# Attention, MLP and routed experts on one core: the sixth pair's product turned, and another order of the first batch's side work

## The chip, the cores and the metric

The kernel runs on one core of a Trainium2 chip. The metric is the device time of one execution in microseconds; the median of three runs of the kernel before is 1160.09 us (1159.63 to 1160.9). Lower is better.

## What is computed

The reference has three stages, one after the other, on 4 batches of 448 tokens:

```
q_n, k_n = rmsnorm(q, g_q), rmsnorm(k, g_k)              # 4 batches, 12 heads, 448 tokens, 64 wide
attn = softmax(q_n @ k_n.T / 8) @ v                      # heads laid side by side: 1792 tokens x 768
h = attn @ w_in;  x = (h * clip(h + 3, 0, 6) / 6) @ w_out    # 768 -> 2048 -> 768, both weights in float64
# capacity routing: every token to one of 8 experts, 224 tokens each
out[tokens of e] = relu(x @ w1[e]) @ w2[e]
```

The two MLP weights come as 64-bit floats and have to be narrowed to 32 bits on the chip. Products that need full precision are made of a high and a low part of each operand.

## The kernel before

**Attention by pairs.** The 48 heads are worked off in 24 pairs, six to a batch; the code counts them from 0, so the sixth pair of the first batch is i = 5. A pair goes through these steps, each a small function: `load` (q and k by DMA), `squares` (ACT, L251), `fold` (POOL, L256, adds the halves of the squares), `sums` (DVE, L267), `guess` (DVE) and `invert` (Newton steps for the inverse root, L279 to L282 on POOL, 12 instructions for a group of two pairs), `norm` (POOL, L298), `transp` (TensorE transposes L315, then `qh` and `kh` on ACT, L324, and the low parts `ql` and `kl` on DVE, L327), `s1` (scores, L338) with the row maxima `mx` on DVE (L341), `mt` (the maxima are transposed, L347, and spread as `mr` on DVE, L349), `sT` (scores transposed, less the maxima, L360) with the exponentials `ph` on ACT (L371).

**Two forms of the last product.** The product with v exists in two forms. In the turned one (`pv`, L449, and `psums`) the exponentials stream 448 wide, the result is copied to `xn_t` on ACT (L452), and the row sums `sm` come from extra matmuls (`L460` in the first batch; in later batches from sums `pa` that POOL adds beforehand, L442 and L465). The sums then make a trip through DRAM: `rs_out` writes `sum_dr`, `rs_in` reads it back as `rs`, `rec` makes the reciprocal `rr` on DVE (L482, L483), `r_out` writes `rec_dr`, `r_in` reads it spread over the partitions into `rb`, `xmul` multiplies on POOL (L497), and `xsplit` gives the high part on ACT (`xh`, L507) and the low part on POOL (`xl`, L505). In the other form (`av`, L400, named QMAJOR) 112 columns of exponentials are the weights and 66 columns stream; the sum falls out of an extra column, `normalize` divides on POOL (L421), and `xt` transposes back (L432). Before, the sixth and the last pair take this form.

**The weights.** `conv` narrows one of 16 column blocks of w_in: part -1 loads it (`wraw`, 768 KB), part 0 is on ACT (L141), parts 1 to 3 on DVE (L142 to L144, `cv`), and a last part stores it (`w<-cv`, 384 KB). The first MLP matrix (`mlp1_atoms`, L559) reads it back as `win_v`, splits it on ACT (L118) and on POOL or DVE (L119), keeps the split for later batches (`w_hl`), and multiplies; `g` leaves through L562 and L564.

**The order.** Nothing is scheduled by a planner. Every step is entered with a number by `at(t, fn, ...)`; the numbers are sorted, and each engine gets its instructions in that order. One pair is 16 places long. MLP matmuls are filled in between from a queue, evenly over the places left of a batch. All DMAs named here go through one queue, SP's, which also issues in that order and holds everything behind a DMA that waits. The constants T_..., TX0 and QMAJOR (L68 to L81) and the loop at L746 to L796 are the whole table.

```
    for i in range(NH // 2):
        t = 16 * i
        at(t + T_LOAD, load, i)
        first = 16 * g[0]
        t_sq = first + T_SUMS + 4 * (i - g[0])
        at(t_sq, squares, i)
        ...
            at(first + (T_INV0 if late_g else T_INV), invert, g)
```

Of the kernel before, what the change touches and what calls it, by code (L numbers as in the profile page):

```python
# [21 lines left out]
def kernel(  # L22
# [15 lines left out]
    B, H, S, D = q.shape  # L38
# [7 lines left out]
    NP = H // 2  # L46
# [21 lines left out]
    CI, CI0, CI1, CI2, CO = 6, 1.75, 2.5, 0.5, 1.5  # L68

    T_LOAD, T_VLOAD, T_NORM, T_Q, T_K, T_V = -72, -12, -38, -30, -28, 6  # L70
    T_SUMS, T_INV, T_INV0, NG0 = -50, -42, -35.5, 10
    T_S1, T_MT = (-24, -23.9, -16, -15.9), -9
    T_ST = (0, 0.1, 8, 8.1)
    T_AV = ((17, 18, 19.5, 20.5), (22, 23, 24.5, 25.5))
    T_NUM, T_XT, T_MLP = 28, 33, (37, 41, 41, 37)
    T_ADD, T_PV, T_SUM = (6, 13), (15.6, 15.62, 15.64, 15.66), 15.7
    T_RS, T_RL, T_REC, T_RO, T_RB, T_X, T_XH, T_XL = 19.5, 21.5, 24, 25.5, 28, 33, 35.5, 39.5
    GD, WD2, C_ST = 12, 8, 5
    TX0 = (20, 23, 27, 29, 32.5, 39, 42, 46)
    QMAJOR = (NP - 1, B * NP - 1)  # L80
    T_CI, D_CI, T_CO, D_CO, T_CL = 20, 10, 180, 12, 14  # L81


    order = ExitStack()
# [652 lines left out]
    def at(t, fn, *args):  # L737
        events.append((t, len(events), fn, args))
# [6 lines left out]

    for i in range(NH // 2):  # L746
        t = 16 * i
        at(t + T_LOAD, load, i)
        at(t + T_VLOAD, vload, i)
        g = GROUP[i]  # L750
        first = 16 * g[0]
        t_sq = first + T_SUMS + 4 * (i - g[0])
        at(t_sq, squares, i)
        if 2 <= i < NG0:
            at(t_sq + 2, fold, i)
            t_sq += 3
        at(t_sq, sums, i)
        late_g = 4 <= g[0] < NG0
        if i == g[-1]:
            at(t_sq if 2 <= i < NG0 else first + T_INV, guess, g)  # L760
            at(first + (T_INV0 if late_g else T_INV), invert, g)
        at(t + (T_INV0 + 0.1 if late_g and i == g[0] else T_NORM), norm, i)
        at(t + T_Q, transp, i, 0)
        at(t + T_K, transp, i, 1)
        at(t + T_V, vsplit, i)
        for c in range(NCH):
            at(t + (T_S1[c] if i else -24 + 0.1 * c), s1, i, c)
            at(t + (T_ST[c] if i else (-9, -8.9, 1, 1.1)[c]), sT, i, c)
            if i in QMAJOR:
                for s in range(2):  # L770
                    at(t + T_AV[s][c], av, i, s, c)
            else:
                at(t + T_PV[c], pv, i, c)
        at(t + (T_MT if i else -21), mt, i)
        if i in QMAJOR:
            at(t + T_NUM, normalize, i)
            at(t + T_XT, xt, i)
        else:
            for n in range(2 if i >= NP else 0):
                at(t + T_ADD[n], padd, i, n)  # L780
            at(t + T_SUM, psums, i)
            tx = TX0 if i < NP else (T_RS, T_RL, T_REC, T_RO, T_RB, T_X, T_XH, T_XL)
            for d, fn in zip(tx, (rs_out, rs_in, rec, r_out, r_in, xmul)):
                at(t + d, fn, i)
            at(t + tx[6], xsplit, i, False)
            at(t + tx[7], xsplit, i, True)
        if (i + 1) % NP == 0:
            at(t + T_MLP[i // NP], mlp_next, i // NP)
# [1 line left out]
    at(8 * H + 2, prefetch, 0)  # L790
    at(8 * H + 14, prefetch)
    for u in range(NF if wide else 0):
        for out_, t in ((0, T_CI + D_CI * u), (1, T_CO + D_CO * u)):
            at(t - T_CL, conv, (out_, u), -1)
            for part in (0, 1, 2, 3, C_ST):
                at(t + part, conv, (out_, u), part)  # L796
# [446 lines left out]
    for pi, (t, hfs) in enumerate(passes):  # L1243
# [10 lines left out]
        for f in range(NF):  # L1254
            i, k = divmod(f, QF)
# [139 lines left out]
```

## Time and profile before

| | |
|---|---|
| median of three runs | 1160.09 us |
| profiled execution | 1162.06 us, its span 1160.2 us |
| busy: TensorE (PE), DVE, ACT, POOL | 95%, 60%, 45%, 40% |
| granted TensorE clock, mean | 0.979 |
| first 58 us: PE busy | 40.42 us |
| 600 us to the end: PE busy | 540.93 of 560.20 us |

The profile is one execution. A row of the view by stretches gives each engine's busy time in that stretch, the granted TensorE clock as a share of 2.4 GHz, and how busy the DMA engines were. A row of the timeline gives start, length, engine, line, what is written and read and how many, and in square brackets the idle time of that engine just before, with what ended it. The trace keeps two records for one 32-bit product of `av` or `sm`, so x16 there are 8 products and x64 are 32.

### The profile page before, as it was taken

The numbers are of one execution on the slowest core, as the hardware profiler recorded it, in microseconds if no ns is written. First come the engines' busy times: TensorE is split into PE (matmuls) and PEld (weight loads), VectorE is DVE, ScalarE is ACT, GpSimd is POOL, SyncE is SP. The second block draws the span as 40 slices with busy tenths as digits, with TensorE's granted clock in tenths as the row PEclk, the third lists the DMA queues.
The fourth block names the chain that finished last, engine by engine and source line by source line (L and its number), as shares of the span: only waits on it lengthen the run. The fifth ranks groups of instructions, "written<-read, shape, count | busy, mean of one in ns | idle before, by whom it ended". The sixth has DMA issues, their size and how long they took to land.

```text
span 1160.2 us, 19232 instructions
## 1 busy us (share of the span) xinstructions
PE 1099.2 (95%) x7073; PEld 880.7 (76%) x7073; DVE 692.2 (60%) x1440; ACT 521.3 (45%) x941; POOL 464.6 (40%) x410
## 2 busy tenths in 40 slices
PE   4978899999999999999999999999997999999997
PEld 3446556766766667787767888888887899999997
DVE  7877877886677845212341666666665846555550
ACT  4655555745545556533542111111114766666551
POOL 4665555664445533112444000000004677775540
PEclk9987989999999999999999999999998999999999
DMA  4575998978777887659996222222237888877731
GB/s 133 145 197 148 248 300 252 309 238 297 251 250 253 257 288 239 222 190 276 356 310 204 78 69 82 64 76 71 70 104 185 245 262 247 248 227 217 226 130 39
DMA packets 215357, 232.17 MB, mean 200 GB/s; under 512 B 28296, under 2 KB 188384, under 8 KB 215264
## 3 DMA queue, kind: packets, MB, share of 16 engines
q1 hardware_dynamic: 211936, 219.94, 61.6%
q0 software_dynamic: 3328, 11.01, 3.1%
q8 instruction: 55, 0.90, 0.3%
q14 instruction: 38, 0.31, 0.1%
HBM read 179.82 MB, written 51.09 MB: 199 GB/s over the span
## 4 chain that ended last, share of the span: by engine, by line
PE 67%; DVE 10%; DMA 9%; issue 5%; POOL 4%; ACT 3%; SPq 1%; POOLq 0%; DVEq 0%; ACTq 0%
PE y L1195 19%; PE h L559 15%; PE y L1347 8%; PE h L1283 5%; PE st L360 4%; PE av L449 4%; PE h L1285 3%; DMA w_hl<-w 2%; DMA we_s<-in_moe_w_dram 2%; DVE mx L341 2%; PE rt L988 1%; PE lg L601 1%; PE sm L465 1%; DMA gr<-g_dr 1%; DVE cv L143 1%
## 5 line engine op out<-in xcount | busy, mean ns | idle before, releaser
L559 PE MATMUL h<-xh,w 128*128 128x448 f32 x768 | 239.9, 382 | 1.0 <-DVE mx L341 0.5
L559 PEld LDWEIGHTS h<-xh,w 128*128 128x128 f32 x768 | 143.3, 191 | 35.9 <-issue 22.1
L559 PE MATMUL h<-xl,w 128*128 128x448 f32 x384 | 145.7, 379 | 0.0
L341 DVE TENSOR_REDUCE mx<-s 112x1 f32<-112x448 f32 x192 | 105.9, 611 | 51.6 <-PE s L338 51.3
L1133 ACT ACTIVATE g2h<-gr 128x512 fp32r<-128x512 f32 x60 | 37.9, 631 | 206.1 <-PE y L1195 161.6
L1195 PE MATMUL y<-woh,g2l 128*128 128x512 f32 (+1 forms) x448 | 124.8, 344 | 1.0 <-POOL g2l L1098 1.0
L1195 PE MATMUL y<-woh,g2h 128*128 128x512 f32 (+1 forms) x448 | 125.3, 345 | 0.0
L1195 PE MATMUL y<-wol,g2h 128*128 128x512 f32 (+1 forms) x448 | 125.2, 344 | 0.0
L1098 POOL TENSOR_TENSOR g2l<-gr,g2h 128x512 fp32r<-128x512 f32 x14 | 19.0, 1361 | 240.6 <-DMA gr<-g_dr 209.0
L119 POOL TENSOR_TENSOR wel<-we_s,weh 128x768 fp32r<-128x768 f32 x48 | 96.3, 2010 | 45.4 <-ACT weh L118 37.0
L118 ACT ACTIVATE weh<-we_s 128x768 fp32r<-128x768 f32 x107 | 88.4, 841 | 57.9 <-DMA we_s<-in_moe_w_dram 39.3
L119 DVE TENSOR_TENSOR wel<-we_s,weh 128x768 fp32r<-128x768 f32 x59 | 78.3, 1334 | 60.3 <-ACT weh L118 53.6
L371 ACT ACTIVATE ph<-st 112x448 f32<-112x448 f32 x192 | 93.0, 545 | 40.8 <-PE st L360 39.7
L442 POOL TENSOR_TENSOR pa<-ph 112x448 f32<-112x448 f32 x68 | 85.6, 1279 | 44.2 <-ACT ph L371 44.2
L1283 PE MATMUL h<-xe,weh 128*128 128x448 f32 x318 | 100.4, 375 | 2.0 <-DVE xe L1234 2.0
L559 PEld LDWEIGHTS h<-xl,w 128*128 128x128 f32 x384 | 73.2, 191 | 11.9 <-issue 7.0
L1195 PEld LDWEIGHTS y<-woh,g2l 128*128 128x128 f32 x448 | 72.0, 189 | 10.7 <-POOL g2l L1098 1.3
L1195 PEld LDWEIGHTS y<-woh,g2h 128*128 128x128 f32 x448 | 71.9, 189 | 10.6 <-issue 1.5
L1195 PEld LDWEIGHTS y<-wol,g2h 128*128 128x128 f32 x448 | 71.9, 189 | 9.1 <-issue 0.7
L1285 PE MATMUL h<-xe,wel 128*128 128x224 f32 x318 | 76.6, 268 | 0.0
L562 ACT ACTIVATE r<-h,half 128x448 f32<-128x448 f32 x64 | 40.6, 634 | 77.7 <-PE h L559 67.3
L497 POOL TENSOR_TENSOR xn_t<-xn_t,rb 128x448 f32<-128x448 f32 x22 | 25.8, 1175 | 119.7 <-DMA rb<-rec_dr 119.7
(252 smaller groups left out, 2386.1 us busy)
## 6 DMA issues: line engine op xcount, KB each, us to landing
we_s<-in_moe_w_dram SPq DMA_DIRECT2D x128, 384.0 KB
w<-w_hl SPq DMA_DIRECT2D x32, 768.0 KB
gr<-g_dr SPq DMA_DIRECT2D x52, 256.0 KB
wraw<-in_moe_w_in_dram SPq DMA_DIRECT2D x16, 768.0 KB
win_v<-w SPq DMA_DIRECT2D x32, 384.0 KB
w_hl<-w SPq DMA_DIRECT2D x16, 768.0 KB
wraw<-in_moe_w_out_dram SPq DMA_DIRECT2D x16, 768.0 KB
g_dr<-g SPq DMA_DIRECT2D x48, 224.0 KB
```

Of the source, the lines that this page charges most:

```text
L118: nc.scalar.activation(hi, raw, AF.Copy)
L119: eng.tensor_tensor(lo, raw, hi.bitcast(F32), op=OP.subtract)
L341: mx = nc.vector.tensor_reduce(MX[i][:, s, c:c + 1], pp[s][:CP, :S], axis=AX.X, op=OP.max)
L360: nc.tensor.matmul(pp[s][:CP, :S], a[r], b[r], start=(n == 0), stop=(n == len(todo) - 1))
L371: nc.scalar.activation(e, pp[s][:CP, :S], AF.Exp)
L442: nc.gpsimd.tensor_tensor(PA[i, s, n], PP[i, s, 2 * n][0], PP[i, s, 2 * n + 1][0], op=OP.add)
L449: nc.tensor.matmul(p[r, :S], vvs[i % 2][:, s, c, V0:V0 + 64], PP[i, s, c][0], start=(c == 0), stop=(c == NCH - 1))
L559: nc.tensor.matmul(p[:, :S], lhs[:, c], x[:, c], start=(n == 0), stop=(n == 3 * NC - 1))
L1195: nc.tensor.matmul(pp[hf][:, :COLS[hf].stop - COLS[hf].start], a[:, f % QF], w[:, COLS[hf]], start=(f == 0 and n == 0), stop=(f == NF - 1 ...
L1283: mm = [lambda: nc.tensor.matmul(p[:, :4 * CP], wh[:, fo], x.rearrange("d k t -> d (k t)"), start=(c == 0), stop=(c == NC - 1), skip_group ...
L1285: lambda: nc.tensor.matmul(p[:, :2 * CP], wl[:, fo], x[:, 0], start=False, stop=False, skip_group_check=True)]
L1347: nc.tensor.matmul(p[:CP, :HW], a[:, f, tk], w[:, o], start=(f == 0 and n == 0), stop=(f == FB - 1 and n == 2))
```

## The change

Only numbers of the table change, and the set of pairs that take the untransposed form.

```diff
-    T_SUMS, T_INV, T_INV0, NG0 = -50, -42, -35.5, 10
+    T_SUMS, T_SQ, T_INV, T_INV0, NG0 = -50, -58.9, -42, -35.5, 10
-    T_NUM, T_XT, T_MLP = 28, 33, (37, 41, 41, 37)
+    T_NUM, T_XT, T_MLP = 28, 33, (39, 41, 41, 37)
-    GD, WD2, C_ST = 12, 8, 5
-    TX0 = (20, 23, 27, 29, 32.5, 39, 42, 46)
-    QMAJOR = (NP - 1, B * NP - 1)
-    T_CI, D_CI, T_CO, D_CO, T_CL = 20, 10, 180, 12, 14
+    GD, WD2, C_ST = 12, 8, 8.5
+    TX0 = (18.5, 22.5, 26.5, 28.5, 33, 40.3, 42, 44)
+    TX1 = (17, 19.5, 22.5, 24, 27, 32, 34, 36.5)
+    QMAJOR = (B * NP - 1,)
+    T_CO, D_CO, T_CL = 180, 12, 12.5
+    T_CI = [16 * i + t for i in range(1, 11) for t in ((8.3, 12.3) if i % 2 == 0 or i > 6 else (8.3,))]
...
-        at(t + T_LOAD, load, i)
+        at(t + (T_LOAD if i < 4 else -68), load, i)
...
-        t_sq = first + T_SUMS + 4 * (i - g[0])
+        late_g = 4 <= g[0] < NG0
+        t_sq = t + T_SQ if late_g else first + T_SUMS + 4 * (i - g[0])
...
-            tx = TX0 if i < NP else (T_RS, T_RL, T_REC, T_RO, T_RB, T_X, T_XH, T_XL)
+            tx = TX0 if i < NP - 1 else TX1 if i < NP else (T_RS, T_RL, T_REC, T_RO, T_RB, T_X, T_XH, T_XL)
...
-        for out_, t in ((0, T_CI + D_CI * u), (1, T_CO + D_CO * u)):
+        for out_, t in ((0, T_CI[u]), (1, T_CO + D_CO * u)):
```

In words: the sixth pair takes the turned product, with its own places for the trip through DRAM (TX1); the first MLP starts two places later; q and k of pairs 4 on are loaded four places later; squares of pairs 4 to 9 stand at one fixed place of the pair, after `kh`; narrowing stands at one or two fixed places of a pair, and its store later; the low part `xl` of the first batch's pairs stands two places earlier.

The first place is TensorE (PE) around the sixth pair's product. Before; `av` of 112x66 is that pair's, `t<-ident,xn` are the transposes of the ninth pair, `t<-ident,mx` the maxima of the eighth:

```order
L338 MATMUL s_1400<-kh,qh 112x448
L338 MATMUL s_1401<-kh,qh 112x448
L400 MATMUL av<-vv_134,ph 112x66 x8
L315 MATMUL t<-ident,xn_1355 128x112 x4
L400 MATMUL av<-vv_134,ph 112x66 x4
L315 MATMUL t<-ident,xn_1357 128x112 x4
L400 MATMUL av<-vv_134,ph 112x66 x12
L347 MATMUL t<-ident,mx_130 128x112
```

After the change, from one block of scores earlier (`av` of 64x448 and `sm` are the sixth pair's):

```order
L451 MATMUL av<-ph,vv_134 64x448 x8
L462 MATMUL sm<-ph,ones_124 32x448 x8
L362 MATMUL st<-qh,kh 112x448 x2
...
L340 MATMUL s_1413<-kh,qh 112x448
L340 MATMUL s_1414<-kh,qh 112x448
L317 MATMUL t<-ident,xn_1351 128x112 x4
L317 MATMUL t<-ident,xn_1353 128x112 x4
L349 MATMUL t<-ident,mx_130 128x112
```

The 32 products of 66 columns (24 in these rows, 8 behind the next scores) are gone, 8 products and 8 sums of 448 columns stand one block of scores earlier, and the transposes follow the scores directly.

The second place is DVE between the maxima of the third and the fourth pair (`mx`; `st_2` are the sums of squares, `cv` the narrowing, `mr` the spread maxima). Before:

```order
L341 TENSOR_REDUCE mx_128<-s_524 112x1
L267 TENSOR_REDUCE st_2_529<-sq 112x8 x2
L327 SCALAR_TENSOR_TENSOR ql<-t,gq_72,qh 128x448
L327 SCALAR_TENSOR_TENSOR kl<-t,gk,kh 128x448
L267 TENSOR_REDUCE st_2_529<-sq 112x8 x2
L271 TENSOR_SCALAR st_2_529<-st_2_529 112x32
L272 TENSOR_SCALAR st_2_530<-st_2_529 112x32
L142 TENSOR_SCALAR cv<-cv 128x768
L143 SCALAR_TENSOR_TENSOR cv<-wraw,cv 128x768
L349 TENSOR_TENSOR mr<-t,place 128x448
L144 SCALAR_TENSOR_TENSOR cv<-wraw,cv 128x768
L341 TENSOR_REDUCE mx_130<-s_592 112x1
```

After:

```order
L343 TENSOR_REDUCE mx_128<-s_527 112x1
L329 SCALAR_TENSOR_TENSOR ql<-t,gq_72,qh 128x448
L329 SCALAR_TENSOR_TENSOR kl<-t,gk,kh 128x448
L351 TENSOR_TENSOR mr<-t,place 128x448
L343 TENSOR_REDUCE mx_130<-s_581 112x1
...
L343 TENSOR_REDUCE mx_130<-s_602 112x1
L269 TENSOR_REDUCE st_2_455<-sq 112x8 x2
L273 TENSOR_SCALAR st_2_455<-st_2_455 112x32
L274 TENSOR_SCALAR st_2_456<-st_2_455 112x32
L144 TENSOR_SCALAR cv<-cv 128x768
L145 SCALAR_TENSOR_TENSOR cv<-wraw,cv 128x768
```

Sums and narrowing have left the stretch between a pair's second four maxima and the `mr` that the scores wait for; they now stand behind the next four maxima.

The third place is the DMA queue SP where the sixth pair's sums go out (`sum_dr`, `rs`, `rec_dr`, `rb` are that pair's trip; `win_v` are the MLP's first three weight blocks, `wraw` the next blocks to narrow). It did not exist before; now:

```order
L473 DMA sum_dr_1422<-rb 4x448
L183 DMA win_v<-w_97 128x6x128 x3
L478 DMA rs<-sum_dr_1422 112x2x8
L238 DMA ld_v<-in_v_dram 112x2x256
L489 DMA rec_dr_1464<-rr 112x8
L495 DMA rb<-rec_dr_1464 64x448 x2
L161 DMA wraw<-in_moe_w_in_dram 128x6x256
```

The read-back `rs` stands behind three blocks of 384 KB.

## Rows read from the trace of the kernel before

**Rows 1.** Busy time by stretch, each from one pair's `mt` to the next; then two single stretches.

```profile
core 0: us, PE busy (x) PEld busy (x) DVE busy (x) ACT busy (x) POOL busy (x), PEclk, DMA share, GB/s
37.50:51.20 13.70, 11.38 (x82) 5.83 (x82) 11.92 (x25) 10.31 (x20) 8.31 (x16) 1.00 0.43 123
51.20:64.40 13.20, 11.38 (x81) 6.03 (x81) 11.85 (x18) 7.58 (x16) 6.66 (x6) 1.00 0.71 185
64.40:82.90 18.50, 14.25 (x81) 7.02 (x82) 12.76 (x25) 8.68 (x17) 11.49 (x19) 0.82 0.72 198
82.90:95.30 12.40, 12.03 (x84) 6.45 (x82) 9.34 (x17) 9.73 (x19) 5.78 (x6) 0.86 0.73 211
95.30:115.40 20.10, 16.91 (x97) 14.01 (x98) 15.73 (x26) 9.88 (x19) 11.78 (x20) 0.72 0.46 124
115.40:135.60 20.20, 17.89 (x104) 10.81 (x104) 15.81 (x24) 12.12 (x24) 10.24 (x8) 0.86 0.96 244
157.90:184.60 26.70, 23.30 (x121) 15.93 (x119) 19.59 (x28) 13.03 (x24) 12.26 (x10) 0.87 0.96 300
102.90:117.70 14.80, 14.69 (x79) 13.24 (x79) 10.50 (x17) 4.90 (x11) 7.71 (x14) 0.54 0.55 147
```

**Rows 2.** Busy time of line L400 (`av`) alone, 104 to 122 us.

```profile
104.00:122.00 18.00, 11.28 (x64) 10.93 (x64) 0.62 0.65 158
```

**Rows 3.** TensorE's timeline: turned products, one set of sums, and one wait.

```profile
69.75 5.01 PE L449 MATMUL av<-ph,vv 112*64 112x448 f32 x16
74.69 1.71 PE L460 MATMUL sm<-ph,ones 112*32 112x448 f32 x16
...
120.81 3.23 PE L449 MATMUL av<-ph,vv 112*64 112x448 f32 x16
...
162.82 0.71 PE L360 MATMUL st<-qh,kh 64*112 64x448 f32 x1 [2.68 <-DVE g L564]
```

**Rows 4.** What TensorE waited for, 37 to 136 us: us in total, times, longest.

```profile
PE t L347 <- DVE mx L341: 3.7, 4, 1.7
PE s L338 <- ACT kh L324: 3.2, 3, 1.5
PE s L338 <- ACT xn_t L452: 2.6, 1, 2.6
PE sm L465 <- POOL pa L442: 2.2, 1, 2.2
PE st L360 <- DVE mr L349: 1.3, 1, 1.3
```

**Rows 5.** ACT's timeline: the copy of the fourth pair's product.

```profile
80.41 0.54 ACT L452 ACTIVATE xn_t<-av 128x448 f32<-128x448 f32 x1 [7.31 <-POOL xl L505]
```

**Rows 6.** The chain that ended last, one piece: start, length, what.

```profile
100.61 7.88 DMA rs<-sum_dr
```

**Rows 7.** POOL's timeline: Newton steps, the low part, normalized rows, one multiplication.

```profile
72.62 0.25 POOL L282 TENSOR_TENSOR st<-st,st 112x32 f32<-112x32 f32 x1
...
74.28 0.95 POOL L282 TENSOR_TENSOR st<-st,st 112x32 f32<-112x32 f32 x1
...
79.25 1.13 POOL L505 TENSOR_TENSOR xl<-xn_t,xh 128x448 fp32r<-128x448 f32 x1
...
101.86 0.24 POOL L279 TENSOR_TENSOR st<-st 112x32 f32<-112x32 f32 x1 [0.33 <-DVE st L272]
...
105.72 1.04 POOL L298 TENSOR_TENSOR xn<-ld_q,st 112x512 f32<-112x512 f32 x1
...
121.77 1.13 POOL L497 TENSOR_TENSOR xn_t<-xn_t,rb 128x448 f32<-128x448 f32 x1 [10.43 <-DMA rb<-rec_dr]
```

**Rows 8.** DVE's timeline: sums of one pair, and one block narrowed.

```profile
68.68 0.74 DVE L267 TENSOR_REDUCE st<-sq 112x8 f32<-112x256 f32 x2
...
73.60 0.52 DVE L142 TENSOR_SCALAR cv<-cv 128x768 int32<-128x768 int32 x1
74.15 0.96 DVE L143 SCALAR_TENSOR_TENSOR cv<-wraw,cv 128x768 int32<-128x768 int32 x1
```

**Rows 9.** The page's costliest groups: matmuls of the first MLP matrix.

```profile
L559 PE MATMUL h<-xh,w 128*128 128x448 f32 x768 | 239.9, 382 | 1.0 <-DVE mx L341 0.5
```

More of the change, by code (lines that the diff above doesn't have):

```diff
@@ L757 @@
         at(t_sq, sums, i)
-        late_g = 4 <= g[0] < NG0
         if i == g[-1]:
```

## The prediction

> **What bounds the kernel now.** I read the views in this order: busy time by stretch, what TensorE waited for, its timeline at the costly places, then the engine or queue that released each wait. From the ninth pair on the MLP fills TensorE; before that attention stands alone and the engine has gaps. Six stretches, each from one `mt` to the next and so one pair long, show how uneven it is [rows 1]: 13.7, 13.2, 18.5, 12.4, 20.1 and 20.2 us, 98.1 together, with TensorE busy 83.8 of them and at a lower clock in four. The reader should see two things there. No other engine is full either (DVE has 11.9 of 13.7 in the first, 15.8 of 20.2 in the last), so this is a chain of waits in fixed orders, not one full engine. And the clock falls after waits and with the sixth pair's product: from 102.9 to 117.7 us TensorE is busy for 14.69 of 14.80 us and is granted 0.54, near the lower of its two levels (1.2 of 2.4 GHz). What follows this stage is TensorE's own work, so time won here should reach the end unless a later wait takes it.
>
> **The change, part by part.**
>
> *Turned product for the sixth pair.* The 32 narrow products took 11.28 us [rows 2]. In their place come 8 wide ones and 8 sums, 3.23 and 1.71 us at the full clock [rows 3], 4.94 together: 6.3 won. The rest of the low-clock stretch, 14.69 - 11.28 = 3.4 us, ran at about half speed, so 1.7 more. I take 8.0. The low end is the product at full clock: 11.28 x 0.62 (the clock in that row) = 7.0, less 4.94, is 2.1.
>
> *Squares behind `kh`.* In every second pair two squares, and the sums they wait for, stood on ACT between `qh` and `kh`. TensorE waited for `kh` three times, 3.2 us [rows 4], and behind one of these waits a turned product took 5.01 instead of 3.23 [rows 3]. 3.2 + 1.8 = 5.0; low end 0, if the maxima are then late by as much.
>
> *Sums and narrowing behind the maxima.* They stood between the maxima and `mr`. `mt` waited 3.7 and the scores 1.3 for `mr` [rows 4]: 5.0; low end 0 for the same reason.
>
> *Low part ahead of the Newton steps.* ACT could not copy the fourth pair's product for 7.31 us [rows 5], as its buffer was held until `xl`, which stood behind 12 Newton steps and two multiplications; TensorE then waited 2.6 [rows 4]. 2.6; low end 0.
>
> *Places of the trip through DRAM.* Loads of 768 KB stood directly ahead of the fifth pair's small transfers: reading back `rs` took 7.88 us [rows 6], POOL waited 10.43 us for `rb` [rows 7], and `pa` was late for TensorE by 2.2 [rows 4]. The loads now stand behind `rs`. 2.2; low end 0.
>
> *Clock.* The stretches with 0.82, 0.86 and 0.86 lose 14.25 x 0.18, 12.03 x 0.14 and 17.89 x 0.14, together 6.8 us [rows 1], of which 1.8 is counted. With most waits gone I take half of the other 5.0: 2.5; low end 0.
>
> Sum of what goes: 8.0 + 5.0 + 5.0 + 2.6 + 2.2 + 2.5 = 25.3. It leaves 72.8 for six stretches, 12.1 each, and the shortest of today is 12.4.
>
> **What is late next.**
>
> *Newton chain.* With the sums of squares behind the maxima, every second pair has `xl` 1.13, sums 0.74, twelve Newton steps 105.72 - 101.86 = 3.86 and `xn` 1.04 in a row [rows 7, 8] before the transposes, 6.8 us. Beside it TensorE has a turned product with sums, 4.94 [rows 3]. Uncovered 1.8, three times: 5.5. Low end 0 (the scores around it cover the rest). The high end takes one row more: a Newton step of 0.25 took 0.95 while DVE narrowed [rows 7, 8]. Two such steps a group make 1.4 more, 4.2 in all: 9.7.
>
> Here a rule speaks against the change. The Trainium skill (SBUF — State Buffer, section "SBUF: two separate sides") says that GpSimd and a VectorE operation with two SBUF inputs share a port pair as an exclusive lock, so that one blocks for the other's whole length. The row of 0.95 us agrees. By it every Newton group now beside narrowing would pay the high end, and the sum would end 4.2 us later.
>
> *Second narrowing in a gap.* Every other gap takes two: 2 x (0.52 + 2 x 0.96) + 0.74 = 5.6 on DVE [rows 8] against 4.94 of cover, three times 0.7: 2.1. Between 0 and three whole ones, 7.3.
>
> *Sixth pair's trip.* Its `rs` stands behind 1152 KB. Behind 768 KB it took 7.88 [rows 6], so up to 11.8. DVE stops at `rr`, and behind it wait `mr` of the eighth pair and the ninth's first maxima; cover is the seventh pair's product (its wide part 3.23 [rows 3]) and the scores around it. I take 3, between 0 (it lands under that cover and the scores) and 8.6 (11.8 less 3.23).
>
> *First MLP later.* Eight matmuls that stood before the ninth pair's `mt` now follow it: 8 x 239.9/768 = 2.5 us [rows 9], between 0 and 8 x 0.382 = 3.1.
>
> At nothing I cost the later loads of q and k (six to nine places ahead of their squares; price below) and the store of a narrowed block three and a half places later, which only frees the queue from waiting for DVE.
>
> Sum of what comes: 5.5 + 2.1 + 3 + 2.5 = 13.1. Net 12.2. The profiled execution took 1162.06, 1.97 above the median of the runs. 1162.06 - 12.2 = 1149.9 on that scale, 1148 as a median.
>
> **The rivals.**
>
> *All new waits are covered* (0.15). Newton chain, second narrowing and the trip fall beside other work: 10.6 less, 1138. For it speaks that DVE is idle for 3 to 6 us in most stretches [rows 1]; against it, that orders which never slip are rare in this trace.
>
> *Newton steps and narrowing hold each other* (0.2). 4.2 more, and the gaps bring back the lower clock, 2.5: 1155.
>
> *The overlapped stage gives it back* (0.06). One block more is narrowed after the MLP starts, 1152 KB; at 300 GB/s, with DMA busy at 0.96 [rows 1], that is 3.8 us of transfers. If weights come late for each block that is still to be narrowed, the gain drains away: 1158 to 1162, no change.
>
> *Loads too late, slower* (0.12). From the twelfth pair on every second pair has its load six places ahead of its squares instead of ten, and behind `rb` in the queue. A place is 26.70/16 = 1.67 us there [rows 1]: 10.0 us instead of 16.7, less what `rb` waits. If the load lands later, ACT stops before `r`, the MLP's bank stays full, and TensorE stands. That happened once for another reason: 2.68 us [rows 3], and 23.30 x 0.13 = 3.0 of clock in that stretch [rows 1], 5.7 together. Seven pairs are exposed; from the third on the gain is gone (3 x 5.7 = 17.1): 1165. Against it speaks that the wait list of TensorE before names no load.
>
> **How the numbers follow.** The forecast, 1148, has 0.47. A measurement of this kernel tells about 0.2%, 2.3 us, from no change. Faster by more: 0.47 + 0.15 + 0.2 = 0.82; within: 0.06; slower: 0.12. The range goes from 1138 (the first rival's time) to 1160, which leaves out the slower case and little else; the bounds of the terms reach beyond it (all at their good ends win 25.3, all at their bad ends lose 26.6), but only if all go one way.
>
> **What would show it.** Right: no L400 before the last batch; the six stretches at 11.5 to 13.5 us, with the clock at 0.9 or more; the wait for `kh` and for `xn_t` gone from TensorE's list. Newton chain: TensorE waits for `xn` at the transposes of every second pair. Trip: one DVE wait at `rr` of more than 4 us, behind `win_v`. Wrong: ACT waits at `sq` for `ld_q` in the overlapped stage, or the stretches shrink and the stage behind them grows by as much.

## The result, and the profile after the change

The changed kernel takes **1176.67 us** (median of 4 runs, 1174.74 to 1178.32) beside 1160.49 of the kernel before (1159.63 to 1166.67), a ratio of 1.0127, 95% interval 1.0087 to 1.0167. It is slower by 16 us in the medians (15 by the ratio) where 12 fewer were forecast, and lies outside the range. Its profiled execution took 1175.33 us, 13.2 us more of span than before.

Busy time by stretch, each row from one `mt` to the next, from the third `mt` to the twelfth, shows where that is lost. Columns: stretch, its length, then busy time and instructions of PE, PEld, DVE, ACT and POOL, the granted clock of TensorE, the DMA share and GB/s.

```profile
40.77:54.10 13.33, 10.65 (x81) 5.78 (x82) 9.88 (x21) 8.44 (x17) 8.12 (x16) 1.00 0.66 182
54.10:68.36 14.26, 10.62 (x84) 5.90 (x82) 13.69 (x22) 10.19 (x19) 5.63 (x6) 1.00 0.36 103
68.36:85.28 16.92, 12.86 (x81) 7.41 (x82) 11.67 (x21) 8.44 (x16) 10.14 (x18) 0.83 0.87 235
85.28:99.58 14.30, 12.33 (x83) 6.86 (x81) 12.70 (x22) 10.31 (x19) 5.84 (x6) 0.85 0.36 104
99.58:116.62 17.04, 13.06 (x81) 7.83 (x82) 10.74 (x21) 8.28 (x16) 10.53 (x19) 0.81 0.87 225
116.62:142.11 25.49, 16.37 (x75) 8.37 (x74) 17.74 (x23) 13.61 (x25) 15.57 (x13) 0.70 0.61 158
142.11:166.51 24.40, 24.40 (x133) 17.98 (x133) 18.63 (x36) 11.39 (x20) 9.90 (x8) 0.89 0.88 253
166.51:194.57 28.06, 22.69 (x120) 15.20 (x118) 16.98 (x25) 12.91 (x23) 11.20 (x9) 0.88 0.84 257
194.57:220.13 25.56, 22.60 (x121) 15.06 (x120) 18.42 (x36) 13.91 (x25) 11.28 (x10) 0.93 0.86 259
```

The first six take 101.3 us where before they took 98.1 [rows 1]. TensorE has less to do in them, 75.9 us against 83.8: the narrow products, 11.28 us, gave way to cheaper ones, and the eight MLP matmuls that now follow the ninth `mt` had taken 1.72. But it stands for 25.4 us instead of 14.3, and the sixth stretch alone takes 25.49 at a clock of 0.70. The three rows behind them lose 6.6 more. From the twelfth `mt` on (13.2 us late) the two kernels run alike.

What TensorE waited for from 20 to 260 us, then ACT and SP's queue from 20 to 225 us (us in all, times, longest):

```profile
PE t L317 <- POOL xn L300: 10.6, 4, 4.1
PE t L349 <- ACT kh L326: 7.2, 1, 7.2
PE t L349 <- DVE mx L343: 5.7, 3, 3.4
PE s L340 <- ACT ph L373: 5.5, 2, 4.8
...
ACT sq L253 <- DMA ld_q<-in_q_dram: 12.5, 4, 3.9
...
SPq L161 <- DVE cv L146: 36.6, 10, 7.6
```

Three of these are new. TensorE waits for `xn` at the transposes, the squares on ACT wait for their load, and SP's queue stands 36.6 us at L161, the load `wraw` of a raw block, until `cv` L146 (the end of a narrowing) has set its buffer free. Before, the queue stood about as long for the narrowing (30.2 us), but at the store of a narrowed block. One passage shows what stands behind the wait now, on SP, ACT, POOL and TensorE (start, length, engine, line, operation, idle time before it and its releaser):

```profile
55.78 0.33 SPq L478 DMA_DIRECT2D rs<-sum_dr  x1
63.80 0.38 SPq L161 DMA_DIRECT2D wraw<-in_moe_w_in_dram  x1
64.27 0.49 SPq L231 DMA_DIRECT2D ld_q<-in_q_dram  x1
64.86 0.41 SPq L231 DMA_DIRECT2D ld_k<-in_k_dram  x1
65.32 0.45 SPq L489 DMA_DIRECT2D rec_dr<-rr  x1
...
70.43 1.12 SPq L495 DMA_DIRECT2D rb<-rec_dr  x2
...
69.87 0.63 ACT L253 ACTIVATE sq<-ld_q 112x512 f32<-112x512 f32 x1 [3.95 <-DMA ld_q<-in_q_dram]
...
74.03 1.13 POOL L499 TENSOR_TENSOR xn_t<-xn_t,rb 128x448 f32<-128x448 f32 x1 [2.04 <-DMA rb<-rec_dr]
75.86 1.14 POOL L507 TENSOR_TENSOR xl<-xn_t,xh 128x448 fp32r<-128x448 f32 x1 [0.69 <-ACT xh L509]
76.96 0.95 POOL L281 TENSOR_TENSOR st<-st 112x32 f32<-112x32 f32 x1
...
83.48 0.82 PE L317 MATMUL t<-ident,xn 112*128 112x112 f32 x3 [4.06 <-POOL xn L300]
```

SP issues nothing from 56.1 to 63.8 us. Then q, k and the reciprocals go out together with a raw block of 768 KB. The squares start 3.95 us late, `rb` lands late, POOL multiplies and makes the low part late, and the Newton steps, now behind the low part, start at 76.96. TensorE stands 4.06 us at the transposes.

The 7.2 us at the ninth `mt` have a longer chain, in which the narrowing is the smaller part (DVE, POOL, SP, ACT and TensorE):

```profile
125.50 2.59 DVE L484 TENSOR_TENSOR rr<-rs 112x8 f32<-112x8 f32 x1 [7.29 <-DMA rs<-sum_dr]
126.26 1.80 POOL L121 TENSOR_TENSOR w<-win_v,w 128x768 fp32r<-128x768 f32 x1
...
133.95 0.50 SPq L231 DMA_DIRECT2D ld_q<-in_q_dram  x1
...
140.04 0.63 ACT L253 ACTIVATE sq<-ld_q 112x512 f32<-112x512 f32 x1 [3.53 <-DMA ld_q<-in_q_dram]
...
142.11 0.42 PE L349 MATMUL t<-ident,mx 112*128 112x112 f32 x1 [7.22 <-ACT kh L326]
```

SP stands from 121.8 to 128.4 us for `rr`, the reciprocals of the sixth pair's trip, and then 1.7 us at `wraw` for a narrowing. `ld_q` leaves behind both, lands some 6 us later, and the squares, which there still stand ahead of `kh`, hold `kh` until 141.49.

### The profile page after: what moved, and what is told of

The parts are those of the page before. It is cut to its first block, busy times and chain, and to the rows that moved or that the text cites. A ratio compares the mean times of both kernels' runs of the same rounds, so it can differ in the third digit from the quotient of the medians.

```text
span 1173.4 us, 19131 instructions
## 1 busy us (share of the span) xinstructions
PE 1094.9 (93%) x7037; PEld 876.4 (75%) x7037; DVE 691.6 (59%) x1438; ACT 522.6 (45%) x941; POOL 458.6 (39%) x411
## 4 chain that ended last, share of the span: by engine, by line
PE 67%; DMA 10%; DVE 10%; issue 5%; ACT 3%; POOL 3%; SPq 2%; POOLq 0%; DVEq 0%; ACTq 0%
PE y L1197 19%; PE h L561 15%; PE y L1349 8%; PE h L1285 5%; PE av L451 4%; PE st L362 4%; PE h L1287 3%; DMA sum_dr<-rb 2%; DVE mx L343 2%; DMA we_s<-in_moe_w_dram 1%; DMA rs<-sum_dr 1%; PE rt L990 1%; PE lg L603 1%; DMA rec_dr<-rr 1%; PE t L317 1%
## 5 line engine op out<-in xcount | busy, mean ns | idle before, releaser
L121 DVE TENSOR_TENSOR wel<-we_s,weh 128x768 fp32r<-128x768 f32 x59 | 81.7, 1393 | 56.9 <-ACT weh L120 43.7
L1197 PEld LDWEIGHTS y<-woh,g2l 128*128 128x128 f32 x448 | 72.1, 189 | 10.6 <-POOL g2l L1100 1.3
L451 PE MATMUL av<-ph,vv 112*64 112x448 f32 x368 | 76.1, 556 | 2.6 <-DVE mx L343 1.3
```

What stands on the lines that cost most here:

```text
L121: eng.tensor_tensor(lo, raw, hi.bitcast(F32), op=OP.subtract)
L451: nc.tensor.matmul(p[r, :S], vvs[i % 2][:, s, c, V0:V0 + 64], PP[i, s, c][0], start=(c == 0), stop=(c == NCH - 1))
L1197: nc.tensor.matmul(pp[hf][:, :COLS[hf].stop - COLS[hf].start], a[:, f % QF], w[:, COLS[hf]], start=(f == 0 and n == 0), stop=(f == NF - 1 ...
```

## The experiments

Theory A: the narrowing's load waits on SP ahead of things that are urgent. Theory B: only the later places of the loads count. Theory C: the new orders on DVE and POOL are too long by themselves. Theory D: the sixth pair's trip through DRAM is late. Each ratio is against the kernel before in the same set of runs (medians there 1161 to 1162).

**1. A third raw buffer (a1_raw3).**

```diff
-            raw = rawp.tile([128, 768, 2], I32, name="wraw", bufs=2)
+            raw = rawp.tile([128, 768, 2], I32, name="wraw", bufs=3)
```

> The changed kernel with a third buffer for the raw block that is narrowed (room for it is made by building the identity in the place of the index table, which the routing builds again), so that the load wraw never waits on SP for the narrowing of the block before last. Theory A (that wait holds the loads of q and k, rec_dr and rb behind it, 36.6 us of queue time from 20 to 225 us, and this makes the squares, the Newton steps and kh late): SP's wait of wraw for cv falls from 36.6 us to under 3, ACT's wait of sq for ld_q from 12.5 us to under 3, and the time falls by 10 to 20 us, to 1157 to 1167. Theory B (the loads of q and k come four places later, whatever stands ahead of them): ACT's wait for ld_q stays above 8 us and the time above 1172. Theory C (the order on DVE and POOL itself, Newton steps and two narrowings in one gap, is too long): SP's wait goes, TensorE's waits for xn (10.6 us) and mx (9.1 us) stay, the time stays above 1170.

The room for the buffer comes from building the identity in the place of the index table, which the routing then builds again. That edit stands in every run here with the third buffer, and in none without it.

1164.02 us, ratio 1.0012 (0.9986 to 1.0037): 12.7 us come back. SP's wait of `wraw` for `cv` falls from 36.6 to 3.0 us, and that of `sq` for `ld_q` is gone. So A holds for most of the loss. Where it comes back is seen from the starts of `mt`: the two kernels are 14.2 us apart at the twelfth, of which 2.1 arise ahead of the third, 3.3 between the third and the ninth, and 8.8 behind the ninth, in the first rows of the MLP. There `wraw` holds SP in the changed kernel for 10.3 of the 36.6 us (142 to 200 us), and the MLP's own transfers `w_hl` and `win_v` leave behind it too. ACT then stands at the split `w`, and TensorE for `ph` behind it; neither wait is in this run, though c1_one6 and c3_both, with the same buffer, still wait 2.5 and 1.7 us for `ph`. The changed kernel:

```profile
172.88 0.84 ACT L120 ACTIVATE w<-win_v 128x768 fp32r<-128x768 f32 x1 [4.83 <-DMA w_hl<-w]
174.72 1.14 PE L340 MATMUL s<-kh,qh 64*112 64x448 f32 x2 [4.82 <-ACT ph L373]
```

But TensorE's wait for `xn` (9.2 us) stays and that for `mx` grows to 14.7, as C said: the gain that was forecast is still missing. Its longest wait, 10.6 us for `mx` at the ninth `mt`, is seen on DVE and POOL of that run:

```profile
121.02 3.59 DVE L145 SCALAR_TENSOR_TENSOR cv<-wraw,cv 128x768 int32<-128x768 int32 x1
...
128.88 0.94 DVE L145 SCALAR_TENSOR_TENSOR cv<-wraw,cv 128x768 int32<-128x768 int32 x1
129.86 4.63 DVE L146 SCALAR_TENSOR_TENSOR cv<-wraw,cv 128x768 int32<-128x768 int32 x1
134.41 2.20 DVE L343 TENSOR_REDUCE mx<-s 112x1 f32<-112x448 f32 x4
...
121.94 1.84 POOL L121 TENSOR_TENSOR w<-win_v,w 128x768 fp32r<-128x768 f32 x1
...
127.86 4.06 POOL L444 TENSOR_TENSOR pa<-ph 112x448 f32<-112x448 f32 x2
131.86 1.81 POOL L121 TENSOR_TENSOR w<-win_v,w 128x768 fp32r<-128x768 f32 x1
```

Two narrowings stand ahead of the maxima, and one step takes 0.94 us or 4.63. The long one ends 0.8 us after POOL's `w`.

**2. The old schedule of the narrowing in the changed kernel (a2_oldconv).**

```diff
-    T_CI = [16 * i + t for i in range(1, 11) for t in ((8.3, 12.3) if i % 2 == 0 or i > 6 else (8.3,))]
+    T_CI = [20 + 10 * u for u in range(NF)]
```

with `C_ST` 5 and `T_CL` 14 again.

> The changed kernel with the narrowing's schedule of before (a block every ten places, load 14 places ahead, store 5 places behind). Theory A: as the third buffer, SP's wait of wraw for cv under 5 us, time 1157 to 1168, unless the narrowing between the maxima and mr costs again what it cost before (3.7 us of waits of mt for mx). Theory B: above 1172. Theory C: the waits for mx fall, and the time falls to below 1165 although the third buffer gave nothing.

1176.44 us, 1.0113 (1.0074 to 1.0152): nothing comes back, against A and C. The queue then stands at the store instead:

```profile
SPq L176 <- DVE cv L146: 29.5, 10, 5.6
...
DVE rr L484 <- DMA rs<-sum_dr: 17.7, 3, 7.4
```

So A was named too narrowly: the raw load need not be the one that waits. That any wait of SP for a narrowing harms, with the loads and trips as the change places them, fits this run but is not shown, since no run takes the wait at the store away. In this run the squares wait for no load. Another reading is left by the parts (5): the turned product alone costs 8.2 us and the squares and trip alone 5.0, together 13.2 of these 14.5.

**3. The loads of q and k back (a3_load72).**

```diff
-        at(t + (T_LOAD if i < 4 else -68), load, i)
+        at(t + T_LOAD, load, i)
```

> The changed kernel with the loads of q and k back at 72 places ahead for every pair. Theory A: the loads then stand ahead of the wraw that waits in some gaps and behind it in others; ACT's wait for ld_q falls by half or more, but rec_dr and rb stay behind the wait, and the time falls by 2 to 6 us only, to 1170 to 1174. Theory B: ACT's wait for ld_q is gone and the time is 1160 to 1166. Theory C: no change, 1174 to 1178.

1167.87 us, 1.0039 (1.0013 to 1.0065): 8.8 us back, between what A and B had said. The queue still stands 40.2 us at `wraw`, but q and k are asked for ahead of it, and the squares wait no more. What stands behind the wait decides, not its length.

**4. `wraw` moved behind the loads, with two buffers (d2_cl95).**

```diff
-    T_CO, D_CO, T_CL = 180, 12, 12.5
+    T_CO, D_CO, T_CL = 180, 12, 9.5
```

> The changed kernel with two raw buffers and its late loads, and only wraw moved: 9.5 places ahead of the narrowing in the place of 12.5, so behind the loads of q and k and rec_dr. If the order in the queue is the cause, SP's wait of wraw falls under 8 us, ACT's wait of sq for ld_q under 4 us, and the time is 1160 to 1168. Rival (wraw then lands late for the narrowing, and DVE or ACT waits for it): the squares do not wait, ACT waits at cv for wraw by 5 us or more, and the time stays above 1170.

1166.38 us, 1.0038 (1.0019 to 1.0057). The queue's wait falls to 8.9 us and 10.3 us come back without a third buffer. The rival's wait for a late `wraw` does not show. Three different edits (a buffer, the loads first, `wraw` later) thus give back 9 to 13 of some 15 us, and have only the queue in common.

**5. The parts alone, on the kernel before (b1_turned, b2_conv, b3_sq).** The first has the turned product with its places (`TX1`) and the later MLP, the second only the narrowing's places, the third only squares, sums and the trip's places (`T_SQ`, `TX0`). One line of each edit:

```diff
+    QMAJOR = (B * NP - 1,)
...
+    T_CO, D_CO, T_CL = 180, 12, 12.5
...
+        t_sq = t + T_SQ if late_g else first + T_SUMS + 4 * (i - g[0])
```

> The kernel before with one part of the change alone: the turned product for the sixth pair, its places of the trip through DRAM, and the first MLP two places later. Theory A: the part is good by itself, 4 to 8 us are won, 1152 to 1156. Theory D (the sixth pair's trip is too late behind the three loads win_v, and DVE stops at rr for 7 us ahead of the next maxima): 1160 or above, with a wait of DVE at rr of 5 us or more and TensorE waiting for mx behind it.

> The kernel before with one part alone: the narrowing's new places (behind the maxima, two in some gaps, load 12.5 places ahead, store 8.5 behind). Theory A (the load wraw now waits on SP for its buffer and holds what is behind it): SP's wait of wraw for cv is 15 us or more, and the time is 3 to 10 us over before, 1165 to 1172. Rival (only the later loads of q and k make this wait harmful, as they stand behind it): they stand ahead of it here, the waits of the squares for ld_q stay away, and the time is 1158 to 1163.

> The kernel before with one part alone: squares behind kh, sums of squares behind the maxima, and the new places of the trip (with xl ahead of the Newton steps); loads, narrowing and the sixth pair's product as before. If the prediction's gains are right, TensorE's waits for kh (3.2 us) and xn_t (2.6 us) go, waits for xn of 4 to 7 us come, and the time falls by 3 to 8 us, to 1154 to 1159. Theory C (the Newton steps behind the low part come too late by themselves): the waits for xn are 8 us or more and the time is 1162 or above.

1170.15 us, 1.0075 (1.005 to 1.0101); 1165.08, 1.003 (1.0012 to 1.0049); 1166.87, 1.0047 (1.0021 to 1.0073). No part helps alone, and the three together, 8.2, 3.2 and 5.0 us in the medians, are about as much as the whole change loses. In the second the queue waits longest of all, 41.3 us at `wraw`, and it costs 3 us in the median, the low edge of what A had said, and nothing in the profiled execution (span 1158.8): there the loads are asked for ahead of it. In the third, the waits for `kh` (0.6 us left) and `xn_t` are gone from TensorE's list as forecast, and `xn` has come, with waits and time as C said:

```profile
PE t L315 <- POOL xn L298: 10.2, 3, 4.5
```

In the first the two stretches of the product take 19.69 and 19.44 us [rows 1: 20.1 and 20.2], and DVE stops at the trip ahead of `mr`, as D said:

```profile
123.36 1.16 DVE L483 TENSOR_TENSOR rr<-rs 112x8 f32<-112x8 f32 x1 [5.36 <-DMA rs<-sum_dr]
```

Its profiled execution is only 2.9 us late at the 23rd `mt` (442.7 us before); the other 6 us come up behind it, where nothing was changed. That part isn't explained.

**6. One narrowing in the gap behind the eighth `mt` (c1_one6, with the third buffer), and the loads back as well (c3_both).**

```diff
-    T_CI = [16 * i + t for i in range(1, 11) for t in ((8.3, 12.3) if i % 2 == 0 or i > 6 else (8.3,))]
+    T_CI = [16 * i + t for i in range(11) for t in ((8.3, 12.3) if i in (2, 4) or i > 6 else (8.3,))]
```

> The changed kernel with the third raw buffer, and the second narrowing taken out of the gap behind the eighth mt (one block is narrowed in the first gap instead). Theory N (after the third buffer the two narrowings, beside the adds pa and the splits of w on POOL, are what keeps DVE from the ninth pair's maxima: 10.6 us of wait there): that wait falls below 4 us, the stretch from the eighth mt to the ninth from 24.7 to 18 to 20 us, and the time is 4 to 6 us under the third buffer's run, 1157 to 1160. Rival (the sixth pair's trip holds it: DVE waits at rr for rs): DVE waits longer at rr, the stretch stays above 23 us, and the time stays at 1163 to 1165.

> The changed kernel with the third raw buffer, one narrowing in the gap behind the eighth mt, and the loads of q and k back at 72 places. If the loads' places cost something by themselves, it is 1 to 4 us under the run without that edit; if the third buffer already takes all of it away (theory A), the two are within 2 us of each other: 1156 to 1160.

The first: 1162.78 us, 1.001 (0.9983 to 1.0036), not the 1157 to 1160 that were expected. The stretch falls from 24.7 to 18.8 us as expected and its wait for `mx` from 10.6 to 4.6, but by the third `mt`, behind the gap that took the block over, the run is 2.2 us behind a1_raw3, and by the eleventh `mt` the run is level with a1_raw3 (1.8 and 1.5 us ahead of the kernel before). The second: **1156.15 us, 0.9951** (0.9934 to 0.9968), faster than both kernels. The loads' places are worth 6.6 us here, more than either expectation. From the sixth pair's trip on the later places are behind `rec_dr`, which waits on SP for `rr` (40.5 us in all in the run with the late loads, 34.2 in the other). How that costs 6.6 us is not shown: in neither run do the squares wait for a load. Of the 7.8 us between the two spans 3.1 lie between the tenth `mt` and the eleventh, 26.65 us at a clock of 0.87 against 23.54 at 1.00.

**7. The same without the third buffer (d1_two).**

> The changed kernel with two raw buffers as it had, the loads of q and k back at 72 places, and one narrowing in the gap behind the eighth mt. SP's wait of wraw for cv stays (30 to 40 us), but q and k are asked for ahead of it. If it is their order in the queue that counts (theory A in the form that fits the runs so far: the wait harms through what stands behind it, the loads first), the time is 1156 to 1160, within 4 us of the same kernel with the third buffer. If the wait harms through rec_dr and rb as well (Newton steps and low parts late), it is 1161 to 1166.

1165.54 us, 1.0034 (1.0011 to 1.0056), with 27.8 us of SP's wait at `wraw`. The third buffer is worth 9.4 us even with the loads ahead of the wait, which fits the second expectation, that `rec_dr` and `rb`, behind the wait too, are a second way in which it harms: POOL waits 20.9 us for `rb` here (20 to 225 us) and 8.7 in c3_both.

**8. Newton steps into POOL's idle time (d3_sums).** The sums go directly behind `mr`, the Newton steps directly behind the multiplication and ahead of `xl`, the rest as in c3_both.

```diff
-    ... T_SQ ... = ... -58.9 ...
+    ... T_SQ ... = ... -59.05 ...
-            at(first + (T_INV0 if late_g else T_INV), invert, g)
+            at(first + (-39.6 if late_g else T_INV), invert, g)
```

> The best kernel so far (third buffer, loads at 72 places, one narrowing in the gap behind the eighth mt) with the sums of squares directly behind mr, ahead of the maxima, and the Newton steps directly behind the multiplication, in the idle time that POOL has before xl. If the Newton chain is what TensorE still waits for at xn (3.1 us three times in the last run), these waits fall under 1 us each and the time falls by 3 to 7 us, to 1149 to 1153. Rival: the low part is then late for ACT's copy of the product, or mx late for mt by what was won, and the time stays at 1154 to 1158.

**1151.73 us, 0.9899** (0.9858 to 0.9941), the best here, beside f2_pref below. TensorE's waits, before this edit and with it:

```profile
PE t L349 <- DVE mx L343: 9.5, 5, 3.5
PE t L317 <- POOL xn L300: 9.2, 5, 3.1
```

```profile
PE t L349 <- DVE mx L343: 7.8, 5, 3.0
PE av L451 <- DVE mr L351: 4.3, 1, 4.3
...
PE t L317 <- POOL xn L300: 0.9, 2, 0.5
```

The wait for `xn` is gone and `mx` is no later. The new wait for `mr` is the sixth pair's trip.

**9. The first MLP two places earlier again (d4_mlp37), on c3_both.**

```diff
-    ... T_MLP = 28, 33, (39, 41, 41, 37)
+    ... T_MLP = 28, 33, (37, 41, 41, 37)
```

> The same best kernel with the first MLP back at 37 places. If the eight matmuls moved behind the ninth mt cost 2.5 us as predicted, the time falls by 1.5 to 3 us, to 1153 to 1155. Rival: the sixth pair's xl is not there yet, TensorE waits for it ahead of the mt, and the time is 1156 to 1160.

1156.34 us, 0.9958 (0.9935 to 0.998): no difference, as the rival said, though not shown to be for its reason.

**10. The old product in the best kernel (f1_oldprod), and its trip ahead of the weights (f2_pref).**

```diff
-    QMAJOR = (B * NP - 1,)
+    QMAJOR = (NP - 1, B * NP - 1)
```

> The best kernel (third buffer, loads at 72 places, one narrowing in the gap behind the eighth mt, sums behind mr and Newton steps ahead of xl) with the old product for the sixth pair (32 narrow products, no trip through DRAM) and the first MLP at 37 places. If the turned product is worth what was predicted once the queue is free (8.0 us, less about 3 for its trip), this is 4 to 8 us slower, 1156 to 1160. Rival (the trip takes all of it, as in the run of that part alone on the kernel before): within 2 us of 1152, or faster.

1160.22 us, 0.9987 (0.9972 to 1.0003): 8.4 us slower than the next kernel, which ran in the same set and has the turned product. The two differ in the MLP's places and the place of `win_v` as well, which are worth 0.2 us in d4_mlp37 and nothing in f2_pref beside d3_sums.

```diff
-    at(8 * H + 2, prefetch, 0)
+    at(8 * H + 4, prefetch, 0)
```

> The same best kernel with the turned product, and the three loads win_v moved from ahead of the sixth pair's rs to behind it. If they are what made rs late (DVE waited 3.9 us at rr, TensorE 4.3 us for mr behind it, and then ran the product in 5.99 instead of 3.23 us), the wait at rr falls under 1.5 us and the time by 3 to 7 us, to 1145 to 1149. Rival: the splits w of the first MLP are then late by as much, and the time stays within 2 us of 1152.

1151.78 us, 0.9903 (0.9882 to 0.9925), no faster than with the loads ahead: the rival's time. Without the edit and with it, TensorE and DVE:

```profile
113.81 5.99 PE L451 MATMUL av<-ph,vv 112*64 112x448 f32 x16 [4.33 <-DVE mr L351]
...
112.58 0.44 DVE L484 TENSOR_TENSOR rr<-rs 112x8 f32<-112x8 f32 x1 [3.88 <-DMA rs<-sum_dr]
```

```profile
109.58 3.23 PE L451 MATMUL av<-ph,vv 112*64 112x448 f32 x16 [0.17 <-DVE mr L351]
123.07 0.45 PE L349 MATMUL t<-jp,mx 112*128 112x112 f32 x1 [3.43 <-DVE mx L343]
...
113.43 2.88 DVE L145 SCALAR_TENSOR_TENSOR cv<-wraw,cv 128x768 int32<-128x768 int32 x1
116.35 2.48 DVE L146 SCALAR_TENSOR_TENSOR cv<-wraw,cv 128x768 int32<-128x768 int32 x1
```

The trip's wait and the slow product are gone (5.99 us in the first row, 3.23 in the other), but the narrowing now falls beside POOL's adds and takes 7.2 us instead of 3.5, and the ninth `mt` waits for the maxima behind it.

Starts of `mt` in the profiled executions, as differences to the kernel before (us), and the spans:

```
             third  sixth  ninth  twelfth  span
before        37.5   82.9  135.6   207.0   1160.2
after         +3.2   +2.4   +6.5   +13.2   1173.4
a1_raw3       +1.1   -1.0   +1.1    -1.0   1161.7
a3_load72     +1.2   -0.7   +1.7    +2.8   1163.9
c3_both       +3.2   -0.4   -6.7    -7.8   1152.6
d3_sums       +4.0   -3.1  -11.4   -10.3   1149.9
f1_oldprod    +4.0   -3.0   -4.8    -4.0   1157.2
```

## Why the prediction was wrong

**The step that failed** is the sentence "At nothing I cost the later loads of q and k ... and the store of a narrowed block three and a half places later, which only frees the queue from waiting for DVE." The queue was not freed. The store moved behind, but the next `wraw` took its place as the one that waits for DVE, and the loads, `rec_dr` and `rb` now stood behind it. The rule to look for what is queued behind a waiting instruction was kept for ACT, DVE and POOL, and not for the one step of the narrowing that issues a load. The term was 0; taking the wait away or the loads out from behind it gives 9 to 13 us back. Each of these edits mends most of the loss, and none by itself brings the gain, which came only with further changes of place (c3_both, d3_sums). The rival "loads too late, slower" (0.12) had the sign and the squares' wait for `ld_q`. Its place was wrong (from the twelfth pair on; the first such wait is at 69.87, behind the fifth `mt`), because it priced the loads behind `rb` and not behind the wait.

Point by point, by the terms:

- *Turned product, 8.0:* at least right in size, 8.4 measured in the best kernel with its trip counted in. On the kernel before alone it won 1.2 in its two stretches. The working mixed two windows: of the 14.69 us (102.9 to 117.7) not 11.28 but 9.49 were that product, so the rest was 5.2 and the term by the same steps 8.9.
- *Squares behind `kh`, 5.0:* the wait for `kh` (3.2 before [rows 4]) falls to 0.6 in a1_raw3. The slow product goes on at another place: 4.92 us at 30.70, behind a wait of 0.90 for `vv`, ahead of which the squares now stand. The wait alone does not decide it: in a1_raw3 the same product took 3.23 behind a wait of 1.02.
- *Sums and narrowing behind the maxima, 5.0:* its low end. `mt` waits for `mx` by 5.7 us instead of 3.7, with the queue mended by 6.0 to 16.5 (d4_mlp37, d2_cl95). The work no longer stands ahead of `mr`, but it stands ahead of the next maxima.
- *Low part ahead of the Newton steps, 2.6, and the Newton chain, 5.5 (0 to 9.7):* the wait for `xn_t` went, and `xn` cost 10.6 us, over the high end. The working took the low part itself as on time. It waits for the multiplication, so for `rb`, and the steps wait for both. d3_sums shows that the order was the cost: 9.2 us of waits become 0.9, and the time falls by 4.4.
- *Places of the trip, 2.2:* the wait for `pa` falls from 2.2 [rows 4] to 0.6 us at the same pairs. Small, and mostly right.
- *Clock, 2.5:* not won. Five of the first seven stretches have 0.70 to 0.89; waits remained in them too.
- *Second narrowing, 2.1 (0 to 7.3):* undersized in the gap behind the eighth `mt`, where the stretch falls by 6.0 us when it goes. A step was counted at 0.96 us and takes up to 4.63 there.
- *Sixth pair's trip, 3 (0 to 8.6):* the sign foreseen, one wait of DVE at `rr` of more than 4 us behind `win_v`, came at 7.29 us, and the loads stood behind it on SP as well. In the best kernel its removal wins nothing, as the narrowing is next.
- *First MLP later, 2.5:* 0.2 in d4_mlp37; no run shows why it costs so little.
- *All new waits are covered:* 1148 less 10.6 is 1137, not the 1138 that bounds the range.

For the six stretches 98.1 - 12.2 = 85.9 us were forecast (with the MLP's term in them). With the queue free and one narrowing moved c3_both takes 88.1, and with the Newton steps moved as well d3_sums takes 82.6. That these lie on either side of the forecast is in part luck, as the terms above were off both ways, and c3_both wins only 5 to 6 of the 12 us.

Of the 3.2 us that the changed kernel loses ahead of the third `mt`, 0.6 stand already at the second, 0.9 are the wait for `vv` and 1.7 the slow product behind it. That product took 4.76 to 4.92 us in the profiled executions of the changed kernel, c1_one6, d3_sums, f1_oldprod and f2_pref, and 3.23 in the eight others with the squares moved, behind waits of 0.89 to 1.02 in all of them. So it follows none of the edits to the queue, and in the profiled executions 1.7 us of what a1_raw3 gives back is this product.

What stays open: the 6 us that b1_turned loses behind 440 us (from the last `mt` to the end it loses 4.7, where every other run stays between -1.6 and +1.9). Then, how much of the loss is the queue's and how much the parts' own, as their three losses alone already make up the whole and the queue waits for narrowings in each of them. And whether a third buffer would help the kernel before, where SP waits 30.2 us for narrowings too: no run has it.

## What to carry to other kernels

Ask of every transfer that a change moves when its buffer comes free: with two buffers, a load issued earlier in its queue waits for the consumer of the block before last, and an in-order queue makes everything behind it wait as well. Put loads that can wait behind those that can't, before paying for another buffer. And when a change of several parts loses, try it with each suspected wait taken away before giving up its parts: here none won alone, and with the queue mended (by a buffer that the kernel before lacks) and the Newton steps moved they won 9 us together.

## What was not expected of the hardware

A narrowing step on VectorE (two operands from SBUF) took 0.91 to 0.96 us where POOL was idle; beside POOL's adds and splits single steps took 4.63, 3.59 and 2.88 us (others there still 0.94), and the two adds `pa` beside it took 4.06 instead of 2.28. Even `rr`, 8 columns wide, took 2.59 us at 125.50 in the changed kernel instead of 0.16 (at 62.50), and ended with POOL's `w` (126.26 + 1.80 = 128.06). The Trainium skill (SBUF — State Buffer, section "SBUF: two separate sides") says that a VectorE operation with two SBUF inputs and GpSimd hold a shared port pair exclusively, one blocking the other for its whole length. The rows [those of a1_raw3 above] agree: the step of 4.63 us began at 129.86 and ended 0.8 us after POOL's `w` (131.86 + 1.81 = 133.67), so it lost to more than one POOL operation in a row: the end of the second `pa` and the whole of `w`. The prediction had weighed this for the Newton steps alone, where the rows show 0.95 and 1.07 us; the larger price was on DVE.
